# Activation sums twice as wide, a weight sum in storage of its own, and an instruction order planned with measured durations, in a fused attention and MLP kernel

## Chip, cores, metric

One core of one Trainium2 chip. The metric is the device time of one execution in microseconds, median over runs. The kernel before takes 218.57 us (218.21 to 218.79, 4 runs). Ratios use runs of the fast state alone. The medians of run 5, and of the kernel before beside runs 1 to 4 and 9 to 11, include one slow run each.

## The reference, cut to what matters

```python
scores = (q @ k.T) / sqrt(64); keep 4 sink tokens and a window of 128
a = softmax(scores); x = a @ v               # 4 x 8 heads x 768 x 64 -> x: 3072 x 512
h = x @ w_in                                 # 512 -> 2048
g = h * (1 / (1 + exp(-1.702 * h)))
out = g @ w_out                              # 2048 -> 512
```

## The kernel before

Tokens go in 12 blocks of 256. For blocks 2 to 10 the last product, `g @ w_out`, is done with seven half-size products instead of eight, in a scheme of Strassen's kind. It costs sums of quarters of `w_out` (once) and of `g` (in every block). `w_out` has 8 chunk pairs; so has `g`.

```python
qk32.append(third[...]); v32.append(third[...])     # loads of block 2 land in `third`
wf = [third[:, 1024*n : 1024*n + 1024].bitcast(FP16)... for n in range(3)]   # weight sums lie over it
wf += ring("wf", 1, ...)
...
def forms_of_w():                                   # weight sums: 4 x 4 instructions of 128x512, fp16
    ...
    # the 1st and 2nd wait for the casts of q, k of block 2, the 3rd for its casts of v
    o_wf[j, n] = plan.any({"POOL": (1110, 1250), "DVE": (450, 550)}, f, deps + (free_qk, free_qk, free_v, [])[n], ...)

def forms_of_g(k):                                  # activation sums, w chunk pairs at a time
    w = OPT_("GW", 2)
    for s in range(0, NS, w):
        # s1 = a21 + a22 (DVE); s2 = s1 - a11 (DVE); a21 = a11 - a21 (POOL); s4 = a12 - s2 (DVE)
        ...
```

Nothing is left to the moment on the chip: while the program is built, a list scheduler gives every operation a planned duration, simulates the engines, and so chooses the order on each engine and, where several engines are allowed, the engine. The chip then runs each engine strictly in that order. A planned duration therefore costs nothing itself, but decides the order.

```python
dur, lat = o.engs[e]          # the planned duration, and the time until others may use the result
...
free[e] = s + dur
```

## Time and profile before

| | before |
|---|---|
| time, median | 218.57 us |
| traced span | 215.9 us |
| matmuls | 2282, of which 19 only warm the clock |
| activation sums | 108 on DVE, 36 on POOL, 128x256 each |

The prediction shows the lines that carry the argument. One figure of my own is used in all that follows, the **lag**: at a time t, the time since the span's start minus the time that the matmuls started so far take at full rate (N columns at N/2.4 + 2 ns, 31 ns for 65 columns, warm-ups 0, packed half-height ones half, packed quarter-width ones a quarter). It grows only where TensorE loses time, by waiting or by a lower clock, and it can be compared between kernels whose matmuls stand in another order, since all do the same work (192.6 us of it).

### The profile page before, as it was taken

How to read it: one execution, taken by the hardware profiler on the slowest of the kernel's cores; microseconds unless marked ns; L12 is line 12 of the kernel's file. 1: busy time of each engine (PE TensorE's matmuls, PEld its weight loads, DVE VectorE, ACT ScalarE, POOL GpSimd, SP SyncE). 2: the span in 40 equal slices, each digit the busy share in tenths (PEclk: the TensorE clock that was granted, in tenths of full speed). 3: DMA queues.
4: the chain of work that ended last, by engine and by line, in shares of the span. 5: the costliest groups of instructions: out<-in, count | busy, mean ns of one | idle time of the engine just before them, and what ended most of it. 6: DMA issues, size and time to landing. Idle time of an engine off the chain costs nothing.

```text
span 215.9 us, 5898 instructions
## 1 busy us (share of the span) xinstructions
PE 208.8 (97%) x2282; PEld 165.1 (76%) x2282; DVE 172.8 (80%) x410; ACT 146.9 (68%) x289; POOL 97.6 (45%) x155
## 2 busy tenths in 40 slices
PE   7989999999999999999999999999999999999993
PEld 2447777576778877888878888988878988988852
DVE  3677858499998899999898999898898879885520
ACT  2698645799987779669579659679479566535420
POOL 3495446698672682391391393393912112111000
PEclk9999999999999999999999999999999999999999
DMA  5999999999937947928968858989674024024043
GB/s 196 341 235 205 207 304 232 325 300 285 203 58 157 280 95 172 276 52 181 256 102 177 232 131 170 256 175 265 163 146 100 5 49 100 2 54 95 0 98 101
DMA packets 65917, 36.60 MB, mean 170 GB/s; under 512 B 27968, under 2 KB 61120, under 8 KB 65888
## 3 DMA queue, kind: packets, MB, share of 16 engines
q1 hardware_dynamic: 60848, 30.19, 57.8%
q0 software_dynamic: 4592, 5.37, 13.1%
q10 hardware_dynamic: 448, 0.66, 1.0%
q8 instruction: 18, 0.29, 0.6%
q14 instruction: 11, 0.09, 0.1%
HBM read 27.56 MB, written 6.29 MB: 157 GB/s over the span
## 4 chain that ended last, share of the span: by engine, by line
PE 63%; ACT 13%; DVE 12%; DMA 4%; issue 3%; POOL 2%; SPq 0%; DVEq 0%; ACTq 0%; POOLq 0%
PE bank L752 26%; PE bank L871 17%; PE bank L781 6%; ACT at L639 5%; DVE gF L847 5%; PE bank L679 4%; ACT v L295 4%; DVE gT L766 4%; PE bank L614 3%; PE bank L983 3%; ACT th L764 2%; DMA qk<-in_q_dram 2%; POOL qk L295 2%; DMA blkT<-qk 2%; DVE at L646 1%
## 5 line engine op out<-in xcount | busy, mean ns | idle before, releaser
L752 PE MATMUL bank<-xT,w_in 128*128 128x256 f16 x768 | 99.6, 273 | 0.4 <-DVE osb L909 0.3
L764 ACT ACTIVATE th<-bank 128x512 f16<-128x512 f32 x96 | 57.6, 603 | 43.8 <-PE bank L752 42.3
L752 PEld LDWEIGHTS <-w_in 128*128 128x128 f16 x768 | 72.6, 98 | 11.8 <-issue 2.2
L766 DVE SCALAR_TENSOR_TENSOR gT<-th,bank 128x512 f16<-128x512 f16 x96 | 65.3, 681 | 16.4 <-ACT th L764 15.4
L847 POOL TENSOR_TENSOR gT<-gT 128x256 f16<-128x256 f16 x36 | 25.4, 708 | 72.2 <-DVE gF L847 47.7
L639 ACT ACTIVATE at<-bank 128x512 f16<-128x512 f32 (+1 forms) x96 | 49.2, 577 | 6.4 <-PE bank L614 6.3
L295 POOL CAST qk<-qk 64x512 f16<-64x512 f32 (+1 forms) x70 | 43.7, 627 | 6.9 <-DMA qk<-in_q_dram 4.1
L871 PE MATMUL bank<-third,gF 128*128 128x256 f16 x144 | 34.3, 273 | 0.0
L871 PE MATMUL bank<-w_out,gT 128*128 128x256 f16 x144 | 34.1, 273 | 0.0
L871 PEld LDWEIGHTS <-gT 128*128 128x128 f16 x288 | 27.6, 98 | 4.0 <-issue 0.9
L646 DVE TENSOR_TENSOR at<-at,bank 128x1024 f16<-128x1024 f16 (+1 forms) x40 | 25.0, 634 | 4.7 <-ACT at L639 4.7
L295 ACT CAST v<-v 64x512 f16<-64x512 f32 (+1 forms) x42 | 25.4, 604 | 0.8
L781 PE MATMUL bank<-w_out,gT 128*128 128x512 f16 (+2 forms) x112 | 23.7, 349 | 0.0
L871 PEld LDWEIGHTS <-gF 128*128 128x128 f16 x216 | 20.8, 98 | 2.8 <-DVE xb L701 0.3
L679 PE MATMUL bank<-v,at 128*128 128x65 f16 x352 | 21.1, 193 | 1.1 <-DVE at L646 0.7
L679 PEld LDWEIGHTS <-at 128*128 128x128 f16 x352 | 17.3, 97 | 3.3 <-DVE at L646 2.1
L871 PE MATMUL bank<-wf,gT 128*128 128x256 f16 x72 | 17.2, 272 | 0.0
L871 PE MATMUL bank<-w_out,gF 128*128 128x256 f16 x72 | 17.1, 272 | 0.0
L847 DVE TENSOR_TENSOR gF<-gT,gF 128x256 f16<-128x256 f16 x36 | 15.7, 437 | 0.6
L701 DVE TENSOR_TENSOR xb<-bank,rcp 128x256 f16<-128x256 f32 x36 | 15.0, 418 | 0.4
L781 PEld LDWEIGHTS <-gT 128*128 128x128 f16 x112 | 9.9, 98 | 7.0 <-issue 0.3
L679 PE MATMUL bank<-vs,ats 128*128 128x65 f16 x128 | 15.0, 193 | 0.0
(66 smaller groups left out, 208.2 us busy)
## 6 DMA issues: line engine op xcount, KB each, us to landing
out_dram<-osb SPq DMA_DIRECT2D x46, 128.0 KB, 2.4
v<-in_v_dram SPq DMA_DIRECT2D x11, 512.0 KB, 6.4
qk<-in_q_dram SPq DMA_DIRECT2D x8, 512.0 KB, 4.8
qk<-in_k_dram SPq DMA_DIRECT2D x8, 512.0 KB, 5.9
w_in<-in_moe_w_in_dram POOLq DMA_DIRECT2D x4, 512.0 KB, 9.0
w_out<-in_moe_w_out_dram POOLq DMA_DIRECT2D x4, 512.0 KB, 12.4
qk<-in_q_dram SPq DMA_DIRECT2D x6, 256.0 KB, 5.1
qk<-in_k_dram SPq DMA_DIRECT2D x4, 256.0 KB, 4.8
```

Source lines behind the costliest of these rows:

```text
L295: {"POOL": nc.gpsimd.tensor_copy, "DVE": nc.vector.tensor_copy, "ACT": nc.scalar.copy}[e](out=out, in_=in_)
L614: nc.tensor.matmul(f32(o_s, 2 * n + i)[:, c : c + w], src[d, j], Q[d].rearrange("d j s -> d (j s)")[:, q0 : q0 + w], start=k >= KM, stop=T ...
L639: nc.scalar.activation(out=A[:, i, 0:W], in_=f32(o_s, 2 * n + i)[:, 0:W], func=AF.Exp, scale=scale)
L646: nc.vector.tensor_tensor(out=A[:, :, 0:W], in0=A[:, :, 0:W], in1=mask(c0, c0 + W).unsqueeze(1).to_broadcast((P, 2, W)), op=ALU.mult,)
L679: nc.tensor.matmul(avp()[:, j, i], a_, v_, start=(n == 0), stop=(n == len(mms) - 1))
L701: nc.vector.tensor_tensor(out=X, in0=avp()[:, :, :, 0:D], in1=rc.to_broadcast((P, 2, 2, D)), op=ALU.mult)
L752: nc.tensor.matmul(f32(holder[0])[:, bass.ts(e, TB)], w_in16[:, c, bass.ts(Fi, P)], X[:, c] if k < KX else X2[:, :, c], start=(c == 0), st ...
L764: o_t = op("ACT", 477, 600, lambda first=first: nc.scalar.activation(out=th[first.places[0]], in_=f32(first), func=AF.Tanh, scale=0.851), ...
L766: o_g[k, s] = op("DVE", 590, 700, lambda first=first, s=s: nc.vector.scalar_tensor_tensor(out=g[:, 2 * s : 2 * s + 2].rearrange("p a t -> ...
L781: nc.tensor.matmul(f32(holder[0])[:, 0:w], g[:, Fi, bass.ts(j, P)], w_out16[:, Fi, c0:c1], start=(Fi == 0), stop=(Fi == NF - 1),)
L847: (nc.gpsimd if eng == "POOL" else nc.vector).tensor_tensor(out=o_, in0=a, in1=b_, op=what)
L871: nc.tensor.matmul(f32(holder[0])[:, bass.ts(half, N)], lhs, rhs, start=fresh and s == 0 and half == what(0)[0][0], stop=s == NS - 1, skip ...
```

## The change

Intent: fewer and larger sums on VectorE, the weight sums off the critical time in which POOL and ACT are crowded, and an order that fits what the chip does. The diff, cut to its core, with options resolved to their values where they are not the point:

```diff
-    wf = [third[...] for n in range(3)]
-    wf += ring("wf", 1, ...)
+    wf = [third[...] for n in range(2)]
+    wf += ring("wf", 2, ...)
...
-        ns = {"POOL": (n / 0.96 + 30, n / 0.96 + 130), "DVE": ..., "ACT": (n / 1.2 + 60, n / 1.2 + 170)}
+        ns = {"POOL": (n / 0.96 + 100, n / 0.96 + 200), "DVE": ..., "ACT": (n / 1.2 + 100, n / 1.2 + 210)}
...
-    for k_ in range(KS + 1, NK):            # KS + 1 = 3: v casts from this block on are on ACT
+    for k_ in range(OPT.get("VK", 4), NK):
...
-            o_t = op("ACT", 477, 600, ... tanh
+            o_t = op("ACT", 490, 610, ... tanh
-            o_g[k, s] = op("DVE", 590, 700, ... product after the tanh
+            o_g[k, s] = op("DVE", 604, 710, ... product after the tanh
...
-        deps + (free_qk, free_qk, free_v, [])[n]
+        deps + (free_qk, free_qk, [], [])[n]
...
-        w = OPT_("GW", 2)
+        w = OPT_("GW", 4)
-        {"POOL": (280 * w, ...), "DVE": (100 * w + 60, ...)},  prio=nominal(k, s + 5) + 3
+        {"POOL": (250 * w + 180, ...), "DVE": (60 * w + 210, ...)},  prio=nominal(k, s + 6) + 3
```

> **What bounds the kernel now.** I read the busy shares first, then the same per stretch of 20 us, then the instruction groups of the line that the change rewrites (the activation sums, line 847), then the timeline of VectorE around one of them, and last who waited for whom.
>
> ```profile
> PE 208.8 (97%) x2282; PEld 165.1 (76%) x2282; DVE 172.8 (80%) x410; ACT 146.9 (68%) x289; POOL 97.6 (45%) x155
> ```
>
> TensorE is busy for 97% of the 215.9 us span. A busy figure can hide slack, so the stretches:
>
> ```profile
> 0.00:20.00 20.00, 17.85 (x179) 9.64 (x180) 12.21 (x43) 13.53 (x31) 12.42 (x26) 1.00 1.00 248
> 40.00:60.00 20.00, 20.00 (x236) 14.14 (x231) 17.18 (x45) 19.10 (x38) 16.18 (x25) 1.00 1.01 261
> 80.00:100.00 20.00, 19.53 (x228) 16.54 (x227) 19.26 (x48) 15.82 (x32) 9.30 (x16) 1.00 0.74 170
> 140.00:160.00 20.00, 19.68 (x211) 16.45 (x209) 18.64 (x44) 13.80 (x29) 13.36 (x22) 1.00 0.84 188
> 200.00:216.00 16.00, 12.44 (x99) 8.78 (x96) 4.30 (x7) 3.99 (x8) 0.00 (x0) 1.00 0.28 67
> ```
>
> The columns after the length are PE, weight loads, DVE, ACT and POOL busy, then the granted clock. Over the nine stretches from 20 to 200 us PE is busy for 178.52 of 180 us: 1.48 us of idleness, all in the five stretches where DVE is at 17.8 to 19.3 of 20. I checked this against the starts of the matmuls: a 256-wide one follows another every 109 ns wherever nothing waits, and the sum of what exceeds the usual spacing of the same pair of kinds is 2.8 us after the 20th microsecond, in a dozen places (the large ones at 78.0, 79.1, 81.8, 88.0, 96.9, 103.3 and 151.0 us, 0.2 to 0.4 us each). The other idle time is 2.15 us in the first 20 us and 3.56 us in the last 16 us, where only the last block's output product and its stores remain.
>
> So in the middle there are at most 1.5 to 2.8 us to win, and what makes them is DVE and ACT running late:
>
> ```profile
> L847 DVE TENSOR_TENSOR gF<-gT x36: 274/291/699, 56.2 to 193.7; 128x256 f16<-128x256 f16 x36
> L847 POOL TENSOR_TENSOR gT<-gT x36: 668/709/792, 56.6 to 194.2; 128x256 f16<-128x256 f16 x36
> L847 DVE TENSOR_TENSOR gF<-gF,gT x36: 258/292/640, 58.6 to 194.1; 128x256 f16<-128x256 f16 x36
> L847 DVE TENSOR_TENSOR gF<-gT,gF x36: 259/292/645, 59.8 to 194.4; 128x256 f16<-128x256 f16 x36
> ```
>
> The sums come in two speeds: median 291, maximum 640 to 699 ns. Of the 108 on DVE, 78 take 285 ns in the mean and 30 take 627 ns; all together 41.0 us. The timeline shows why:
>
> ```profile
> 90.70 0.29 DVE L847 TENSOR_TENSOR gF<-gT 128x256 f16<-128x256 f16 x1
> 91.03 0.29 DVE L847 TENSOR_TENSOR gF<-gF,gT 128x256 f16<-128x256 f16 x1
> 91.36 0.64 DVE L847 TENSOR_TENSOR gF<-gT,gF 128x256 f16<-128x256 f16 x1
> ...
> 91.14 0.71 POOL L847 TENSOR_TENSOR gT<-gT 128x256 f16<-128x256 f16 x1 [1.52 <-PE bank L871]
> ```
>
> The third DVE sum starts during the POOL sum and ends 0.15 us after that one does: it was held up, not slowed.
>
> ```profile
> PE bank L679 <- DVE at L646: 0.7, 3, 0.3
> ```
>
> PE waits on DVE only where a mask comes late. At 151.0 us a held-up sum (150.42, 0.64 us) stands just ahead of such a mask (150.99), and PE stops 0.44 us for it.
>
> **What the Trainium skill says.** "SBUF — State Buffer", section "Who interferes with whom": a DVE instruction with two SBUF inputs contends with a GpSimd one that reads SBUF, and whoever is first keeps the port for its whole instruction. The trace agrees: 285 against 627 ns. "VectorE: DVE Perf Modes", section on the TRN2 errata: a fixed latency is paid per instruction, so larger tiles amortize it. It agrees: the uncontended 128x512 weight sums of line 826 take 415 ns, the 128x256 sums 291 ns, so 256 more elements cost 124 ns and some 167 ns are fixed. "TensorE: Matmul & The Clock Gate", section "Back-to-back issue gap", gives N/2.4 + 2.5 ns, 109 ns for 256 columns; the chain shows eight of them in 0.87 us, the same. "Perfetto Trace Analysis", section "Identifying the Most-Contended Engine", warns that matmul busy time is no measure of headroom; that is why I counted starts.
>
> **The change, part by part.**
>
> (1) Four chunk pairs per activation sum. Nine blocks (2 to 10) have four groups of three DVE sums and one POOL sum now, two groups after. No matmul is added or removed. On DVE 108 instructions of 256 columns become 54 of 512. Uncontended: 54 x 415 = 22.4 us, against 108 x 285 = 30.8. Contended: a POOL sum of 128x512 takes 1153 ns (line 826 on POOL). Following the order of the timeline above, the third sum starts 0.33 us after its POOL partner and ends 0.15 us after it, so some 0.97 us, an excess of 0.55. Before, the excess was 41.0 - 30.8 = 10.2 us over 36 groups, 0.28 each, 80% of the full 0.35; 80% of 0.55 over 18 groups is 7.9 us. Sum: 22.4 + 7.9 = 30.3 us, so DVE loses some 11 us, 1.2 us a block. The 34 ns between chained sums are saved 54 times, 1.8 us of idle time more. POOL goes from 36 x 708 = 25.4 us to 18 x 1153 = 20.8. Nearly all of this lies beside matmuls.
>
> (2) Own storage for the third weight sum. Its four instructions no longer wait for the casts of v of block 2 (39.6 to 42.2 us on POOL). Three ran on POOL or DVE at 43.2, 45.9 and 47.0 and one at 50.4, when both were crowded; POOL idles 3.7 us just before 39.6. They move there, if the planner does as the priorities say. Nothing is saved, but some 2.3 us of POOL and 1.3 us of DVE work leave the stretch 43 to 52.
>
> (3) v of block 3 is cast on POOL, not ACT: 4 x 619 = 2.5 us leave ACT between 46.5 and 50.2 us, just where ACT has 19.1 of 20 us, and 4 x 612 = 2.4 us go to POOL, in the place that (2) frees. PE is busy all through this stretch, so the gain here is 0 to 0.3 us.
>
> (4) New planned durations and a later priority for the sums. These cost nothing; they change the fixed order on each engine. They fit the trace better: planned 60w + 210 gives 330 ns for two pairs and 450 for four, the trace has 291 + 34 = 325 and 415 + 34 = 449; before, 260 was planned, so each chained sum ran 65 ns late against the plan, and the mask behind it too. That drift is what the stalls at 78 to 103 and at 151 us look like. The order of the start changes as well, because ACT and POOL casts are planned longer.
>
> Sum: of the 1.5 to 2.8 us of stalls I take half away, 1.1 us; the 40 to 60 stretch 0.1; the first 20 us 0, with 0.6 either way. 218.6 - 1.2 = 217.4 us.
>
> **Rivals.** First, DVE is taken for the bound: a saving of 11 us there would give some 208 us. For it speaks DVE at 19.26 of 20 in one stretch; against it, that PE loses 0.47 us in that very stretch. It cannot give more than the stalls. I give it next to nothing. Second, the wider sums hurt: a held-up DVE sum now blocks DVE for 0.97 us instead of 0.64, and masks queued behind it come later, as at 151 us. If half of the 18 groups stopped PE for 0.3 us more, that is 2.7 us, 221 us. The planner, which now knows the durations but not the hold-ups, can put it either way. Third, nothing: the stalls only move to other places, since the order is planned without the port; 218.6. Fourth, the start: other engines for the first casts move the first matmuls by up to 0.6 us, 218 to 219.2 without the rest.
>
> **Range and chances.** The floor is the before time less all stalls in the middle, 218.6 - 2.8 = 215.8; I put the low end a little above it. The high end allows the third rival and a bad start. Faster by over 2% needs 214.2, below that floor, so only a shorter start and no stalls together could do it: 3%. Slower by over 2% needs 223, more than the second rival at its estimate: 2%.
>
> **What would show it.** DVE busy near 162 us with 54 sums at line 847, uncontended ones at 415 ns and the held-up ones near 0.9 to 1.0 us; POOL near 95, ACT near 144 us. PE busy unchanged but for a few tenths (208 to 209 us), and its idle time from 20 to 200 us below 1 us. Wrong if DVE does not fall by 8 to 13 us; if PE idle in the middle stays at 1.5 us or grows though DVE falls; or if the time moves by more than 3 us, which the middle cannot give, so the start or the end would have to.

## The result, and the profile after

Ratios here and below are the mean time of one kernel's fast runs over that of the other's of the same rounds, so not quite the ratio of the medians that are quoted.

| | before | changed | changed, timed again |
|---|---|---|---|
| median | 218.57 us (4 runs) | 217.46 us (4 runs) | 217.38 us (6 runs; before beside it 218.30) |
| ratio to before (95%) | | 0.9949 (0.9925 to 0.9974) | 0.9966 (0.9940 to 0.9993) |

The gain is 0.3 to 0.5%, 0.7 to 1.1 us, and real: both intervals end below 1. The busy line of the page after:

```profile
PE 208.0 (97%) x2282; PEld 165.5 (77%) x2282; DVE 166.4 (77%) x354; ACT 145.6 (68%) x288; POOL 97.0 (45%) x140
```

DVE lost 6.4 us, TensorE's busy time hardly moved. The stretch from 20 to 200 us, first before, then changed, then the changed kernel's second trace (columns: length, PE, weight loads, DVE, ACT, POOL, clock, DMA):

```profile
20.00:200.00 180.00, 178.52 (x2009) 146.67 (x2007) 156.31 (x361) 129.36 (x252) 85.23 (x129) 1.00 0.74 170
```
```profile
20.00:200.00 180.00, 178.77 (x2031) 148.23 (x2029) 150.83 (x310) 127.87 (x250) 85.16 (x115) 1.00 0.76 171
```
```profile
20.00:200.00 180.00, 178.91 (x2029) 148.37 (x2026) 150.64 (x309) 128.16 (x251) 85.31 (x115) 1.00 0.76 170
```

TensorE is as busy as before in this stretch and gets 20 to 22 more matmuls through: what was won is starts, not busy time. The first 20 us went the other way:

```profile
0.00:20.00 20.00, 17.24 (x162) 8.88 (x163) 10.96 (x38) 13.59 (x31) 11.84 (x25) 1.00 0.98 237
```

162 matmuls stand against 179 before. The second trace of the changed kernel has 175 there, so most of this differs from run to run. The activation sums after:

```profile
L847 DVE TENSOR_TENSOR gF<-gT x18: 394/424/692, 58.9 to 193.3; 128x512 f16<-128x512 f16 x18
L847 POOL TENSOR_TENSOR gT<-gT x18: 1152/1182/1327, 59.4 to 193.8; 128x512 f16<-128x512 f16 x18
L847 DVE TENSOR_TENSOR gF<-gF,gT x18: 415/425/1356, 60.4 to 193.7; 128x512 f16<-128x512 f16 x18
L847 DVE TENSOR_TENSOR gF<-gT,gF x18: 412/681/1259, 61.7 to 194.2; 128x512 f16<-128x512 f16 x18
```

The free ones take 394 to 427 ns, 16 of 54 are held up, for up to 1356 ns. The sum of their durations is 30.0 us, against 41.0 before.

### The profile page after: what moved, and what is told of

Its sections match the earlier page's. It is cut to its first block, busy times and chain, and to the rows that moved or that the text cites. A ratio compares the mean times of both kernels' runs of the same rounds, so it can differ in the third digit from the quotient of the medians.

```text
span 215.4 us, 5785 instructions
## 1 busy us (share of the span) xinstructions
PE 208.0 (97%) x2282; PEld 165.5 (77%) x2282; DVE 166.4 (77%) x354; ACT 145.6 (68%) x288; POOL 97.0 (45%) x140
## 4 chain that ended last, share of the span: by engine, by line
PE 71%; DMA 9%; DVE 8%; SPq 3%; ACT 3%; issue 2%; POOL 2%; ACTq 0%; POOLq 0%; DVEq 0%
PE bank L752 31%; PE bank L871 20%; PE bank L781 9%; DMA w_out<-in_moe_w_out_dram 7%; PE bank L679 5%; PE bank L614 4%; DVE gF L847 3%; DVE gT L766 2%; DMA vs<-in_v_dram 2%; SPq L417 2%; ACT at L639 1%; DVE xb L701 1%; SPq L352 1%; DVE at L646 1%; ACT v L295 1%
## 5 line engine op out<-in xcount | busy, mean ns | idle before, releaser
L766 DVE SCALAR_TENSOR_TENSOR gT<-th,bank 128x512 f16<-128x512 f16 x96 | 65.1, 683 | 16.1 <-ACT th L764 14.4
L295 POOL CAST qk<-qk 64x512 f16<-64x512 f32 (+1 forms) x70 | 44.8, 642 | 13.4 <-DMA qk<-in_q_dram 10.7
L847 POOL TENSOR_TENSOR gT<-gT 128x512 f16<-128x512 f16 x18 | 22.1, 1227 | 63.7 <-DVE gF L847 61.6
L871 PE MATMUL bank<-wf,gT 128*128 128x256 f16 x144 | 27.0, 272 | 0.0
L295 ACT CAST v<-v 64x512 f16<-64x512 f32 (+1 forms) x38 | 22.9, 602 | 0.8
L781 PE MATMUL bank<-w_out,gT 128*128 128x512 f16 (+2 forms) x112 | 23.0, 349 | 0.1
L614 PEld LDWEIGHTS <-blkT 64*128 64x128 f16 x256 | 8.0, 94 | 8.1 <-issue 6.2
## 6 DMA issues: line engine op xcount, KB each, us to landing
w_in<-in_moe_w_in_dram POOLq DMA_DIRECT2D x4, 512.0 KB, 10.8
```

The source lines that it names most:

```text
L295: {"POOL": nc.gpsimd.tensor_copy, "DVE": nc.vector.tensor_copy, "ACT": nc.scalar.copy}[e](out=out, in_=in_)
L614: nc.tensor.matmul(f32(o_s, 2 * n + i)[:, c : c + w], src[d, j], Q[d].rearrange("d j s -> d (j s)")[:, q0 : q0 + w], start=k >= KM, stop=T ...
L766: o_g[k, s] = op("DVE", 604, 710, lambda first=first, s=s: nc.vector.scalar_tensor_tensor(out=g[:, 2 * s : 2 * s + 2].rearrange("p a t -> ...
L781: nc.tensor.matmul(f32(holder[0])[:, 0:w], g[:, Fi, bass.ts(j, P)], w_out16[:, Fi, c0:c1], start=(Fi == 0), stop=(Fi == NF - 1),)
L847: (nc.gpsimd if eng == "POOL" else nc.vector).tensor_tensor(out=o_, in0=a, in1=b_, op=what)
L871: nc.tensor.matmul(f32(holder[0])[:, bass.ts(half, N)], lhs, rhs, start=fresh and s == 0 and half == what(0)[0][0], stop=s == NS - 1, skip ...
```

## The experiments

Twelve runs, on the chip in four groups, with one trace each; each was timed in five rounds against the kernel before (6 runs against 11). The two theories at the start: **the parts pay** (the width, or the measured durations, or the storage carries the gain; W, P and S in the expectations), and **the order pays** (any new order moves the time by some tenths of a per cent or more, whatever it costs; O).

One thing disturbs these ratios. Of the 30 runs of experiments 3, 5, 8, 9 and 10, 14 had a granted clock of 0.991 to 0.992 over the whole run and the others 0.998 or more; all five traces are of the lower kind, and show the clock at 0.50 for 3.4 us. The kernel before had 0.984 to 0.990 in 4 of its 44 runs, and two of these, beside experiments 5 to 8, count as fast. Plain means over the runs above 0.995 alone (3 to 11 a side, no interval) give 1.010 for run 3, 1.007 for run 5, 0.998 for run 6, 1.000 for run 7, 1.010 for run 8, 1.005 for run 9 and 1.003 for run 10; the other ratios hardly move.

### 1. The width alone

```diff
 kernel before
-        w = OPT_("GW", 2)
+        w = OPT_("GW", 4)
```


> The kernel before with one thing changed: sums four chunk pairs wide. The order is planned with the old formula, which for four pairs says 460 ns a DVE sum and 1120 a POOL sum, close to the truth. If the width is what gains (theory W): DVE busy at the sums falls from 41 to about 30 us and the time to 217.5 us or lower, ratio 0.995 or less. If the measured durations in the plan are what gains (theory P): DVE falls the same way, but the time stays within 0.3% of before. If any new order moves the time by some tenths of a per cent (theory O, chance of the order): the time may go either way by up to 1 us, and the places of the stalls change.

218.53 us against 218.60, ratio 0.9997 (0.9970 to 1.0024). DVE fell from 172.8 to 164.5 us busy, and it bought nothing.

### 2. The planned durations alone

```diff
 kernel before
-  the old durations of casts, tanh, product and sums
+  the new ones; width 2 and storage as before
```


> The kernel before with only the planned durations of the change (casts, tanh, the product after it, the sums), still two pairs wide and with the old storage. Theory W: DVE busy stays near 173 us and the time within 0.3% of before. Theory P: the stalls between 60 and 110 us shrink and the time falls by 0.4% or more. The longer planned casts should also reproduce the late start of the changed kernel: PE busy in the first 20 us near 17.2 instead of 17.85 us, some 0.6 to 0.8 us lost; then the time could even be a little above before.

219.55 us, ratio 1.0037 (1.0009 to 1.0066): slower, though the work is the same (two instructions more on ACT and two fewer on POOL, by the page). The later priority of the sums is not part of this run. DVE is at 171.3 us, and the first 20 us have 17.35 us of PE.

### 3. The old plan for the first casts

```diff
 changed kernel
-  o_cqk, o_cv of blocks 0 and 1: cast(...) with the new durations
+  o_cqk, o_cv of blocks 0 and 1: cast(...) with the old durations
```


> The changed kernel, but the casts of blocks 0 and 1 are planned with the old durations, so that their engines and order are those of before. In the changed kernel the first 20 us hold 17 matmuls fewer and some 0.8 us are lost there. If the longer planned casts are the cause, PE busy in the first 20 us comes back to about 17.8 us and the whole is 0.5 to 0.8 us faster than the changed kernel, some 216.8 us, ratio to before about 0.991. If the lost start is made up for elsewhere anyway (the middle has slack at 60 to 80 us), the time stays at 217.5.

220.83 us, ratio 1.0121 (1.0078 to 1.0164). The early start came back as expected (PE 17.92 us in the first 20; the lag there is 10.8 us, but the changed kernel's second trace has 10.9, so this may be the run and not the order), and was lost several times over: TensorE waits 1.92 us at 42 us and 2.23 us at 85 us, and the lag rises by 4.2 us between 40 and 50 us and by 3.7 between 80 and 90. The expectation was wrong about the whole: two constants in the plan of the first casts (70 ns more on POOL, 40 on ACT), which cost nothing, decide over 3 us later on, a part of it slow clock.

### 4. The sums made thin

```diff
 changed kernel, wrong result on purpose
-  tensor_tensor(out=o_, in0=a, in1=b_, op=what)
+  n_ = P if k < 4 else 16
+  tensor_tensor(out=o_[:, :, 0:n_], in0=a[:, :, 0:n_], in1=b_[:, :, 0:n_], op=what)
```


> Wrong result on purpose: the changed kernel in the same order, but from block 4 on each activation sum handles 16 of 128 columns of each chunk, so both DVE and POOL sums become short and barely hold each other up. DVE loses some 15 us more than the change took away. If TensorE bounds the kernel and only its stalls can be won (my prediction), the time falls by at most the stalls that are left in the middle, 1.8 us by the count of starts: 215.7 to 217.2 us. If DVE bounds it, the time falls by 5 us or more, below 212.5.

216.84 us, ratio 0.9924 (0.9900 to 0.9947), relative error 1.3 as meant (blocks 2 and 3 keep full sums, so that both buffers are filled once and no matmul reads memory never written). DVE lost another 11.8 us and POOL 14.3, with the order kept:

```profile
PE 207.7 (97%) x2282; PEld 165.3 (77%) x2282; DVE 154.6 (72%) x354; ACT 145.4 (68%) x288; POOL 82.7 (39%) x140
```

The time fell by 0.5 us against the changed kernel. So DVE's load is not what bounds it; with nearly free sums this order gives some 0.25% more.

### 5. The storage alone

```diff
 kernel before
-    wf = [third[...] for n in range(3)]; wf += ring("wf", 1, ...)
+    wf = [third[...] for n in range(2)]; wf += ring("wf", 2, ...)
-    deps + (free_qk, free_qk, free_v, [])[n];  v casts on ACT from block 3
+    deps + (free_qk, free_qk, [], [])[n];      v casts on ACT from block 4
```


> The kernel before with only the third weight sum in storage of its own (no wait for block 2's v casts) and block 3's v cast on POOL instead of ACT. Width alone gave nothing (0.9997) and the durations alone cost 0.4%, so if one part carries the gain of 0.5% (theory S) it is this one: ratio 0.995. If the parts matter only through the order that they happen to give (theory O), the ratio can lie anywhere between 0.992 and 1.01, and the stalls stand in other places than in either kernel.

221.30 us, ratio 1.0094 (1.0031 to 1.0156). A part of the change costs about 1% by itself. It is the storage together with the move of block 3's v casts; the two were not tried apart, here or in run 7. Its timeline on DVE (line 827 are the weight sums, 767 the product after the tanh), then what POOL and PE do beside it:

```profile
36.70 2.62 DVE L827 TENSOR_TENSOR third<-w_out,third 128x512 f16<-128x512 f16 x2
39.24 1.71 DVE L827 TENSOR_TENSOR wf<-w_out,third 128x512 f16<-128x512 f16 x2
40.87 0.41 DVE L827 TENSOR_TENSOR third<-w_out,third 128x512 f16<-128x512 f16 x1
41.20 0.82 DVE L827 TENSOR_TENSOR third<-w_out 128x512 f16<-128x512 f16 x1
41.95 0.68 DVE L767 SCALAR_TENSOR_TENSOR gT<-th,bank 128x512 f16<-128x512 f16 x1
...
37.70 2.63 POOL L827 TENSOR_TENSOR wf<-w_out 128x512 f16<-128x512 f16 x2
...
42.68 0.29 PE L595 MATMUL bank<-blkT,ks 128*32 128x256 f16 x4 [2.25 <-DVE gT L767]
```

The freed third sums go to POOL at 37.7 us, while DVE does the others. Both read two tensors in SBUF, and where they overlap three DVE sums take 1.3 us each instead of 0.415, and the two POOL sums 1.33 instead of 1.15. The product that TensorE needs stands behind them in the fixed order and comes at 41.95; TensorE idles 2.25 us. Then its clock drops:

```profile
40.00:42.00 2.00, 0.43 (x3) 0.09 (x1) 2.00 (x5) 0.60 (x1) 1.25 (x3) 1.00 0.92 326
42.00:44.00 2.00, 1.32 (x19) 0.79 (x19) 1.97 (x5) 0.67 (x2) 1.88 (x3) 1.00 0.97 291
44.00:46.00 2.00, 2.00 (x15) 0.73 (x14) 1.43 (x3) 2.00 (x5) 1.94 (x5) 0.54 1.14 299
46.00:48.00 2.00, 2.00 (x18) 1.32 (x15) 1.08 (x2) 2.00 (x5) 1.88 (x5) 0.60 1.16 292
```

The last but two column is the granted clock: 0.54 and 0.60. The record has it at 0.50 from 44.17 to 47.58 us, 3.41 us, at half rate an estimated 1.7 us lost. This is not in every run: the three with the clock at 0.998 or more take 219.96 us in the mean, against 222.56 for the other three. The lag rises from 11.6 us at the 40th microsecond to 16.1 at the 50th. The runs old_start and old_durations show the same waits (1.92 and 2.26 us at 42 us) and the same drop.

### 6. Two pairs wide again

```diff
 changed kernel
-        w = OPT_("GW", 4)
+        w = OPT_("GW", 2)
```


> The changed kernel with the sums two pairs wide again, everything else as changed. If the wide sums are needed for the gain together with the rest (theory W+), it is lost: 218.5 us or more, ratio 1.000 or more, DVE near 172 us busy. If they are not needed, it stays near 0.995.

217.78 us, ratio 0.9957 (0.9912 to 1.0003), DVE at 172.1 us. The interval holds the first expectation's 1.000 only at its very end, and the second's 0.995; by the times alone, the width is not shown to matter.

### 7. The storage undone

```diff
 changed kernel
-  two weight sums over `third`, no wait for v, v casts on ACT from block 4
+  three weight sums over `third`, the third waits for v, v casts on ACT from block 3
```


> The changed kernel with the old storage of the third weight sum and block 3's v cast on ACT again. Theory S: the gain is lost, ratio 0.999 to 1.004 (it is then width plus durations, of which one gave nothing and one cost 0.4%). Theory O: anywhere from 0.992 to 1.01.

218.30 us, ratio 0.9973 (0.9923 to 1.0024). The ratio lies just below the range of theory S and inside that of theory O, which excludes little; the interval leaves both. Without the two runs of the kernel before at a clock of 0.99 it is 1.000, inside S, so this run does not tell them apart. The trace shows one thing more: weight sums at 47.58 and 48.74 us are held up (1.04 and 1.17 us) ahead of a copy, and TensorE idles 0.90 us at 50.17 for it. With the storage of the change these sums are over by 43.5 us.

### 8. The durations undone

```diff
 changed kernel
-  the new planned durations, priority s + 6
+  the old ones, priority s + 5; wide sums and own storage stay
```


> The changed kernel with the old planned durations and the old priority of the sums: it is wide sums plus own storage. If the measured durations contribute (theory P), it is slower than the changed kernel, 0.998 or more. If they only spoil the start, as durations_only suggests (lag of 11.9 us at the 20th microsecond against 10.6), it is faster than the changed kernel, 0.992. Theory O: no rule.

220.96 us, ratio 1.0103 (1.0048 to 1.0159), with the wait and the slow clock at 42 us as in run 5. So the storage needs the new durations: with them the order has the product before the held-up weight sums, without them behind. By run 3 the durations of the first casts are enough to make this difference.

### 9 and 10. All weight sums on DVE

```diff
 run 3 (start_wdve), and the changed kernel (after_wdve)
-  o_wf[j, n] = plan.any({"POOL": (1110, 1250), "DVE": (450, 550)}, ...)
+  o_wf[j, n] = plan.any({"DVE": (450, 550)}, ...)
```


> The kernel of the run old_start (changed kernel with the old plan of the first casts) with all 16 weight sums on DVE, none on POOL. In old_start, storage_only and old_durations, DVE weight sums of 1.3 to 1.4 us, held up by POOL weight sums, stand ahead of one product on DVE; TensorE waits 1.9 to 2.3 us for it at 42 us and then runs at a clock of 0.50 for some 3.4 us. If that hold-up is the cause (theory H): no weight sum on DVE above 0.8 us, no PE idle over 0.5 us between 40 and 46 us, clock 1.00 there, the lag at 50 us falls from 16.0 to about 12, and the time from 220.8 to 217.5 or less; with the early start kept (10.8 at 20 us) perhaps 217.0, level with or better than the changed kernel. If not H: the wait at 42 us stays over 1 us.

> The changed kernel with all 16 weight sums on DVE. It has no wait over 0.4 us there, so H gives it nothing to win but the two held-up weight sums (2 x 0.9 us of DVE): ratio to before 0.992 to 0.998. Theory O (any new order moves the time by up to 0.5%): 0.99 to 1.003.

start_wdve: 220.21 us, ratio 1.0070 (1.0043 to 1.0098). after_wdve: 219.64 us, 1.0064 (1.0033 to 1.0094). The local part of the expectation held in start_wdve (one sum of 0.83 us is just over the 0.8): between 40 and 46 us PE is busy throughout at clock 1.00, and the lag at 50 us is 12.8 instead of 16.0. The hold-up is the cause of the wait at 42 us. In both traces five weight sums stand between the product before and the product that TensorE needs; they take 1.23, 1.37, 1.37, 0.41 and 0.41 us in old_start and 0.42 each in start_wdve. DVE in old_start (the last four of them), then in start_wdve (the last three):

```profile
38.23 1.37 DVE L829 TENSOR_TENSOR third<-w_out,third 128x512 f16<-128x512 f16 x1
39.52 1.70 DVE L829 TENSOR_TENSOR wf<-w_out,third 128x512 f16<-128x512 f16 x2
41.15 0.41 DVE L829 TENSOR_TENSOR third<-w_out,third 128x512 f16<-128x512 f16 x1
41.48 0.67 DVE L769 SCALAR_TENSOR_TENSOR gT<-th,bank 128x512 f16<-128x512 f16 x1
```
```profile
37.82 0.76 DVE L829 TENSOR_TENSOR third<-w_out,third 128x512 f16<-128x512 f16 x2
38.49 0.42 DVE L829 TENSOR_TENSOR wf<-w_out,third 128x512 f16<-128x512 f16 x1
39.35 0.69 DVE L769 SCALAR_TENSOR_TENSOR gT<-th,bank 128x512 f16<-128x512 f16 x1 [0.44 <-ACT th L767]
```

But the time is hardly better (expected were 217.5 us or less), since another wait took its place. The same wait puts after_wdve outside both of its expected ranges. In start_wdve:

```profile
40.00:46.00 6.00, 6.00 (x68) 3.70 (x67) 5.65 (x13) 5.60 (x12) 4.44 (x7) 1.00 0.95 298
80.00:82.00 2.00, 0.02 (x1) 0.04 (x1) 2.00 (x4) 1.98 (x5) 0.97 (x1) 1.00 0.76 167
82.00:84.00 2.00, 1.80 (x24) 1.36 (x24) 1.98 (x4) 1.93 (x5) 0.00 (x0) 0.91 1.13 213
84.00:86.00 2.00, 2.00 (x12) 1.40 (x10) 0.30 (x1) 1.98 (x5) 0.39 (x2) 0.50 0.94 214
```

```profile
82.20 0.29 PE L597 MATMUL bank<-blkT,ks 128*32 128x256 f16 x4 [2.18 <-ACT at L642]
```

The order puts two groups of score products almost next to each other, the second waits until ACT has taken the first out of PSUM, and the kernel's own planner foresees it: printing its planned TensorE times while building gives, for the idle times over 0.15 us after 18 us,

```
changed         0.49 us in all; one of 0.31 at 64.4 us
storage_only    1.31 us in all; 0.74 at 40.6 us, 0.57 at 64.8
start_wdve      3.04 us in all; 2.50 at 77.8 us
after_wdve      2.73 us in all; 2.50 at 77.6 us
```

against 2.18 and 2.13 us measured at 82 us. The wait of storage_only at 42 us is planned as 0.74 us and became 2.25: the planner knows the durations, but not that DVE and POOL hold each other up. A planned wait does not foretell one either: the kernel before has the same 0.74 us at 40.6 us in its plan, and its trace has TensorE busy for 20.00 us from 40 to 60.

### 11. The fourth activation sum on DVE too

```diff
 changed kernel
-  a21 = a11 - a21 on POOL
+  a21 = a11 - a21 on DVE
```


> The changed kernel with the fourth activation sum on DVE too, none on POOL. If POOL sums hold DVE up as the timeline suggests, 72 sums on DVE cost about what 54 cost now: 72 x 0.425 = 30.6 us against 30.0, with hold-ups left only from POOL casts. DVE busy stays within 2 us of 166.4, POOL falls by 22 us, and the time stays within 0.4% of the changed kernel. If the POOL sums were a real relief for DVE, DVE rises by 7 us and the time by 1 us or more.

216.88 us, ratio 0.9931 (0.9906 to 0.9955). DVE is at 170.2 us, 3.8 more than in the changed kernel, between the two expectations: the 72 sums take 36.6 us, not 30.6, because POOL's other work still holds some up (maximum 1272 ns). POOL falls by 21.7 us. The time beats the kernel before, and its median is the lowest of all that compute the right result; its interval overlaps the changed kernel's, so that it beats that one is not shown.

### 12. The changed kernel once more

> The changed kernel itself, unaltered, timed in five rounds and traced a second time. The first comparison rests on four runs (ratio 0.9949, interval 0.9925 to 0.9974), and the other readings rest on one trace each. If the gain is real, the ratio is 0.993 to 0.997 with an upper end below 1. If the stalls belong to the order and not to the moment, the trace shows the same ones again: about 0.3 us before the attention products at 68 us, 0.2 us at 80 us, 0.3 us at 102 us, and a lag within 0.3 us of the first trace at every mark (11.4 at 20 us, 14.0 at 70, 19.1 at 200).

217.38 us, ratio 0.9966 (0.9940 to 0.9993). TensorE's idle times over 0.15 us after the 20th microsecond, in the first and the second trace:

```
first    0.33 at 67.95 (attention)   0.23 at 80.03 (scores)   0.27 at 102.17   0.20 at 149.56
second   0.33 at 67.19 (attention)   0.23 at 79.27 (scores)   0.26 at 101.39   0.19 at 148.78
```

They are the same waits of the same length, shifted by the 0.8 us by which the second run was ahead. The waits belong to the order. The lag at 20 us was 10.9 instead of 11.4, so the expected 0.3 us did not hold for the start, which varies, nor for the later marks, which carry this on (13.4 instead of 14.0 at 70 us, 18.4 instead of 19.1 at 200).

### What the lags say together

Growth of the lag in us per stretch, from one trace of each kernel:

```
                 wide  new durations   20-60   60-100   100-200
before            no        no          1.55     3.07      4.33
storage_only      no        no          5.48     2.66      4.61
width_only        yes       no          1.65     2.75      4.44
old_durations     yes       no          5.71     2.98      4.39
durations_only    no        yes         2.38     2.28      4.47
after_width2      no        yes         1.82     2.64      4.55
changed           yes       yes         1.61     2.31      3.79
changed_again     yes       yes         1.33     2.31      3.79
old_storage       yes       yes         3.23     2.61      3.82
old_start         yes       yes         5.71     4.39      3.85
start_wdve        yes       yes         2.19     5.30      3.74
after_wdve        yes       yes         1.39     4.97      3.74
after_all_dve     yes, DVE  yes         1.28     1.77      4.33
thin_sums         thin      yes         1.25     2.31      3.24
```

From 100 to 200 us the kernels that compute the right result fall into two groups with nothing between. Where the wide sums and the new durations come together (POOL keeping its share), 3.74 to 3.85; where one of the three is missing, 4.33 to 4.61. Neither alone helps there, both together win 0.5 to 0.6 us. From 20 to 100 us, where weight sums, casts and first blocks crowd the engines, the order decides, by over 4 us from 20 to 60 and over 3 from 60 to 100; some 1.7 us of this is slow clock in the five traces that have it.

What stands behind single waits can be read too. In the kernel before, four of the large ones (82, 88, 104 and 151 us) come after a sum held up to 0.64 us with the late mask next in DVE's order. In the changed kernel none comes so after 100 us, but three of its four waits over 0.15 us (at 67.95, 102.17 and 149.56, 0.80 us together) have a DVE sum held up to 1.26 to 1.36 us just ahead of the mask or the product that TensorE waits for. The last of them:

```profile
147.47 1.15 POOL L847 TENSOR_TENSOR gT<-gT 128x512 f16<-128x512 f16 x1 [1.65 <-DVE gF L847]
147.55 1.35 DVE L847 TENSOR_TENSOR gF<-gF,gT 128x512 f16<-128x512 f16 x1
148.83 0.67 DVE L766 SCALAR_TENSOR_TENSOR gT<-th,bank 128x512 f16<-128x512 f16 x1
```

## Why the prediction was right

It gave 217.4 us; measured were 217.46 and 217.38. That it is so close is in part luck: the middle gave a little more than expected, the start took some of it, and single parts (runs 1, 2 and 5) gained nothing by themselves.

- **TensorE bounds the kernel and only its stalls can be won**: right. Thin sums took 11.8 us more off DVE and gave 0.5 us (run 4); width_only took 8.3 off and gave nothing.
- **Half of 1.5 to 2.8 us of stalls, 1.1 us**: right in size, though not all its readings were. The idleness before lies in four of the five stretches that it names (120 to 140 us has DVE at 18.22 and TensorE at 20.00), and late masks are four of the six waits over 0.1 us from 20 to 200 us, 0.83 of 1.32 us of idle time; the other two are for sums of the output on DVE. The lag grows by 8.95 us from 20 to 200 us before, by 7.71 and 7.43 in the two traces of the changed kernel: 1.2 to 1.5 us won. The excess over the usual spacing fell from 2.8 to 1.8 us. In the sense of the two groups above, half of what thin sums show to be there after 100 us (4.33 to 3.24) was taken. The mark of less than 1 us of TensorE idle time from 20 to 200 us was missed: 1.23 and 1.09 us, against 1.48 before.
- **The first 20 us, 0 with 0.6 either way**: 0.3 and 0.8 us lost in the two traces. How much of this is the order and how much the run stays open; there is one trace of the kernel before.
- **Activation sums 30.3 us, free ones 415 ns, held-up ones near 0.97**: 30.0 us and 394 to 427 ns. The held-up ones are of two kinds, eleven at 0.54 to 0.72 us and five at 1.26 to 1.36; none is near 0.97, so the right sum is luck.
- **DVE down by 11 us to 162**: wrong, 166.4. The step that failed is equating the summed durations with busy time. Durations did fall by 9.9 us (11.0 at the activation sums, 1.8 back at the weight sums), but neighbouring DVE instructions overlap in the trace, by 19.0 us in all before and 15.6 after: with fewer instructions, less is counted twice. "Perfetto Trace Analysis", section "Optimizing Scalar/DVE Operations", has the reason: the fixed data-access part of an instruction shows at about twice its busy time in a profile, since one half of it overlaps with the next instruction. The trace agrees: overlapping neighbours overlap by 81 ns in the median before and 82 after, about half of the 167 ns of fixed time that the prediction estimates. It did not hurt, as DVE is not the bound. My mark "wrong if DVE does not fall by 8 to 13 us" was set on the wrong quantity.
- **Which part gains**: I put the gain to fewer late masks through width and durations, and nothing to the storage. Width and durations together do gain after 100 us, in one trace of each kernel, but each alone gives nothing there; that the gain is all late masks is not shown. The storage was mis-sized: not 0, but a cost of 4.5 us of lag from 40 to 50 us where the order is unlucky (some 1.7 of it slow clock), and in the changed kernel probably a gain, since the sums at 48 us that cost old_storage 0.90 us are out of the way; the times do not settle it (run 7).
- **The second rival**, held-up sums that delay TensorE, did not win in the changed kernel, though it is behind three of the four waits left there. Runs 3, 5 and 8 show it at full size, through the weight sums, at 220.8 to 221.3 us. I had put the chance of a slowdown over 2% at 2%; with the two constants of run 3 as they were, the same change would have come out 1.2% slower, so this was nearer than I thought.
- **The spacing of matmuls**: the prediction leaves out that "TensorE: Matmul & The Clock Gate", section "Back-to-back issue gap", gives its formula for an isolated matmul and other figures for a stream. This trace, a stream, has 109 ns at 256 columns and 216 at 512, as the formula says.

## What to carry to other kernels

Where TensorE is full, unloading another engine pays only the stalls that this engine causes; count them from the starts of the matmuls before hoping for more. In a fixed order, a part of a change can cost by itself and pay only together with another, so undo parts singly and look at each stretch of the trace, not at the total alone. A planner that knows durations but not which engines hold each other up can put two-input sums on DVE and POOL side by side, and an urgent instruction behind them pays for it.

## What the Trainium skill lacked or had wrong

- "TensorE: Matmul & The Clock Gate", section "HAM oscillation — how this bites in real kernels": its rule is no TensorE idle gap over some 3.4 us. Here idle times of 1.92, 2.13, 2.18, 2.25 and 2.26 us each were followed, from 0.3 us before to 1.5 us after work resumed, by a clock of 0.50 that lasted 3.41 us; one of 2.23 us (old_start, at 85.57) was not, and in these traces none up to 0.90 us was. So much shorter gaps can be enough, and not every one is. Nor does the same order always bring the drop: 16 of the 30 runs of the five kernels with it in their traces kept a clock of 0.998 or more.
- No page says that freeing an operation from a wait can slow a program whose order is fixed beforehand; here it cost 0.9%, or 0.7% over the runs without the slow clock (storage_only, in which block 3's v casts moved too).
